# Attention and expert products on one core: another place and bank for the third chunk's second group, and other ranks for the weight conversions

## The chip, the cores and the metric

The kernel runs on one core of a Trainium2 chip. Its engines are TensorE (PE in the profile), VectorE (DVE), ScalarE (ACT), GpSimd (POOL) and SyncE (SP), which here issues the transfers. Each runs its instructions in the order in which they were issued, and semaphores order the engines among each other. The metric is the device time of one execution in microseconds, less being better; times are medians of several runs, and the profile is of one execution.

## The reference

Four sequences of 768 positions, eight heads of 64. Each query sees the keys nearer than 16 positions and, besides, 24 block summaries: a block of 32 keys is represented by its maximum, a block of values by its mean, and log 32 is added to such a score. The result, 3072 rows of 512, goes through two products with 1536 columns, which are multiplied elementwise, and one product back to 512.

```python
k_sum = k.reshape(B, H, nb, block, D).max(axis=3)
v_sum = v.reshape(B, H, nb, block, D).mean(axis=3)
scores_l = scale * np.matmul(q, k.transpose(0, 1, 3, 2))
mask_l = np.abs(pos[:, None] - pos[None, :]) < window
scores_s = scale * np.einsum('bhsd,bhnd->bhsn', q, k_sum) + np.log(block)
a = softmax(concatenate([where(mask_l, scores_l, -1e9), scores_s]))
x = matmul(a, concatenate([v, v_sum]))
...
a = x @ w_a
b = x @ w_b
return (a * b @ w_out).astype(np.float32)
```

(The softmax is written in one line here; the rest is the reference's.)

## The kernel before

**Chunks and groups.** The 3072 rows are cut into 12 chunks of 256 rows (`u` = 0 to 11, three for each sequence), and a chunk into two groups of 128 queries (`i` = 0, 1). Chunk `u` of attention leaves its result in one of two input buffers, `xs[u % 2]`, as a high part and a low part (`x0`, `x1`, halves per group). The expert products of a chunk are 12 items `(u, f)`, one for each 128 hidden columns: 24 matmuls for the two hidden products (L932) and, one item later, 6 for the product back (L968), with two passes of ACT and two of DVE between them (L949 to L957). The items run `(0, f)` and `(1, f)` interleaved, `(0, 11)`, `(1, 10)` and `(1, 11)` last; then `(2, 0)` and on, chunk by chunk. `x0` holds chunk 0's input until `(0, 11)` has read it; then chunk 2's is written there.

**Weights.** The weights arrive as 64-bit numbers, two words each, in 36 parts that are handled in 18 pairs `j`. A conversion of pair `j` (`convert`, L266) takes, for each half, one ACT pass from the raw words into PSUM bank c0 (L289), three DVE steps that go through banks c0 and c1 (L297, L304, L310), an ACT cast (L342) and two POOL passes (L347, L353). All conversions share c0 and c1, so they follow one another. The intermediate numbers lie in scratch spaces: for pairs 0 to 13 in spaces W15 to W17 and S0, for the last four pairs in three slots of two 512-column places each, which are used in rotation, half by half. The raw words of pairs 15, 16 and 17 are loaded into W15, W16 and W17 once these serve no conversion any more; a load further waits for the conversion four pairs earlier.

**Attention.** For chunks 2 and up a group's steps are: queries transposed on DVE (L881), scores on PE into two banks (L583), scaled and masked by DVE into `s` (L608), row maxima (L616), exponentials and sums on ACT (L628), two small DVE steps (L637, L643), scaling on POOL (L658), twelve 32x256 transposes on DVE from `s` into `pt` (L698), products with the values on PE (L712), and the split of the result into a high part by ACT (L720) and a low part by DVE (L723). The place `pt` (`pbuf`) is one for both groups; four of its sixteen blocks stay zero in every group. Chunk 2 (`FILL`) is worked while weights are still being converted: `next(third)` emits its load of queries behind conversion 7, its first group's scores and transposes behind conversion 9, its second group's scores behind conversion 17, and the rest behind item `(0, 11)`. There both groups' products go to bank c0, the second's scores to c0 and c1.

**The next sequence.** Chunk 3 begins a new sequence. Its keys (`prep_keys`, DVE passes L470 to L491) overwrite `kT` after the last scores of chunk 2. Its value means (`prep_values`) are made by POOL (L513) from loads into S1.0 and S1.1, added up in S0.3 and brought into order in S0.2; from there two transfers carry them into `vw`. A space `S0` or `S1` has four places of 512 columns, S0.0 to S0.3.

**The order.** No order is written by hand. Every step is entered in a list (`Work.add`) with its engine, a rank, an estimated duration and the keys that it reads and writes; a step depends on the earlier steps in the list with which its keys collide. `emit` then plays the engines through with the estimates and issues, engine by engine, the step of the lowest rank among those that are ready within 0.15 us; equal ranks are settled by the time at which they became ready. Ranks are 0 for the passes of the expert products, 2 + `j`/4 for conversion `j` (its ACT cast 0.5 less), 2.3 for chunk 1, 5 for chunk 2 (`SOON`), 5.5 for the next keys (`PREP`) and 6 for later chunks and their value means (`LATER`). PE's scores and products of attention have rank -1.

Of the kernel before, what the change touches and what calls it, by code (L numbers as in the profile page):

```python
# [84 lines left out]
def attention_moe(  # L85
# [10 lines left out]
    nc = tc.nc  # L96
    B, H, S, D = q.shape
    P = 128
# [11 lines left out]
    G = CH // P  # L110
    CV = 512
    NW = 3 * NF // 2
    AHEAD = (7, 9, 17)
    FILL = 2

    const = ctx.enter_context(tc.tile_pool(name="const", bufs=1))
# [60 lines left out]
    pbuf = sb([P, 2, NP, P], "pt")  # L177
    vbuf = [sb([P, H, D], f"vw{e}") for e in range(2)]
# [15 lines left out]
    spaces = {n: sb([P, 2048], n) for n in ("S0", "S1")}  # L194
    for j in (*range(8, 13), *range(NW - 3, NW)):
        spaces[f"W{j}"] = wp.tile([P, 2048], F32, tag=f"W{j}", name=f"space{j}")

    kins = [kin, spaces["S1"][:, 2 * CV : 2 * CV + S + 32]]

    def slot(space, i):  # L200
# [18 lines left out]
    def pool(rank, takes, reads, writes, fn):  # L219
        work.add("POOL", rank, takes, 0.1, reads, writes, fn)  # L220
# [8 lines left out]
    CHAIN, FIRST, CONVERT, NEXT, SOON, PREP, LATER = 0, 1, 2, 2.3, 5, 5.5, 6  # L229
# [31 lines left out]
            "SP", rank, 0.45, 524.0, [f"done{j - 4}"] if j > 3 else [], writes, fn, rate=340  # L261
        )

    slots = [("S0", 0), ("S0", 2), ("S1", 2)]

    def convert(j):  # L266
        rank = CONVERT + j / 4
        rk = [f"raw{2 * j}", f"raw{2 * j + 1}"]

        if j < NW - 4:  # L270
            space = {12: "W16", 13: "W17"}.get(j, ("W17", "W16", "W15", "S0")[j % 4])
            places = [(space, 0, 2), (space, 1, 3)]
            single = j < 2
        else:
            places = [slots[(2 * (j - NW + 4) + h) % 3] for h in range(2)]
            places = [(n, x, x + 1) for n, x in places]
            single = True
        cols = [[slice(x * CV, (x + 1) * CV) for x in xs] for _, *xs in places]
        fx, px = [[spaces[places[h][0]][:, cols[h][x]] for h in range(2)] for x in range(2)]
        fk, pk = [[f"{places[h][0]}.{places[h][1 + x]}" for h in range(2)] for x in range(2)]  # L280
        spans = [(h,) for h in range(2)] if single else [(0, 1)]

        def scale(h):
            high = raws[j][:, 2 * h * CV : 2 * (h + 1) * CV].rearrange("p (n t) -> p n t", t=2)
            nc.scalar.activation(  # L289
                bank["c0"], high[:, :, 1].bitcast(F32), AF.Prelu, scale=2.0**-112, alpha=-(2.0**32)  # L290
            )


        def step(n, h):
            f, p, e, s = fx[h], px[h], bank["c0"], bank["c1"]
            if n == 0:
                nc.vector.tensor_scalar(  # L297
                    out=f.bitcast(I32), in0=e.bitcast(I32), scalar1=3, scalar2=None,
                    op0=ALU.logical_shift_left,
                )  # L300
            elif n == 1:


                nc.vector.tensor_scalar(  # L304
                    out=s.bitcast(I32), in0=f.bitcast(I32), scalar1=-(1 << 23), scalar2=None,
                    op0=ALU.bitwise_and,
                )
            else:
                low = raws[j].rearrange("p (n t) -> p n t", t=2)[:, h * CV : (h + 1) * CV, 0]
                nc.vector.scalar_tensor_tensor(  # L310
                    out=p, in0=low.bitcast(U32), scalar=2.0**-52, in1=s, op0=ALU.mult, op1=ALU.mult
                )

        for n, h in [(n, h) for h in range(2) for n in range(3)]:
            f, p, e, s, r = [fk[h]], [pk[h]], ["c0"], ["c1"], [rk[h]]
            if n == 0:
                act(CHAIN, 0.52, r, e, lambda h=h: scale(h))
            reads, writes = ((e, f), (f, s), (r + s, p + [f"done{j}"] + r))[n]
            dve(rank, 0.6, reads, writes, lambda n=n, h=h: step(n, h))

        def parted(part):
            if j not in homes:
                homes[j] = wp.tile([P, 8, 2, P], F32R, tag=f"W{j}", name=f"w{j}")
            return homes[j][:, :, part, :]

        for hs in spans:
            ms = slice(4 * hs[0], 4 * (hs[-1] + 1))
            f, p, hi, lo = (
                [x[h] for h in hs] for x in (
                    fk, pk, [f"hi{2 * j}", f"hi{2 * j + 1}"], [f"lo{2 * j}", f"lo{2 * j + 1}"]  # L330
                )
            )
            x0 = spaces[places[hs[0]][0]]
            f8, p8 = (
                x0[:, cols[hs[0]][x].start : cols[hs[-1]][x].stop].rearrange(
                    "p (m n) -> p m n", n=P
                )
                for x in range(2)
            )
            act(  # L340
                rank - 0.5, 0.25 + 0.37 * len(hs), f + rk, hi,
                lambda ms=ms, f8=f8: nc.scalar.copy(out=parted(0)[:, ms], in_=f8),  # L342
            )
            takes = 0.2 + 1.1 * len(hs)
            pool(
                rank + 0.1 * hs[0], takes, hi, f,
                lambda ms=ms, f8=f8: nc.gpsimd.tensor_tensor(  # L347
                    out=f8, in0=f8, in1=parted(0)[:, ms].bitcast(F32), op=ALU.subtract
                ),
            )  # L350
            pool(
                rank + 0.1 * hs[0], takes, f + p, lo,
                lambda ms=ms, f8=f8, p8=p8: nc.gpsimd.tensor_tensor(  # L353
                    out=parted(1)[:, ms], in0=f8, in1=p8, op=ALU.add
                ),
            )
# [307 lines left out]
    def transposes(u, t, s, sk, banks, diag=None):  # L664
        rank = rank_of(u)
        if u < FILL:
            d, dk = diag

            def turned(h):
                for c in range(NP):  # L670
                    nc.tensor.matmul(
                        bank[banks[h]][:, c * P : (c + 1) * P], s[h][:, c, :], d[:, h, c, :],
                        start=True, stop=True,
                    )

            for h in range(2):
                pe(
                    -1, 0.85, [f"{sk[h]}{c}" for c in range(NP)] + dk[h], [banks[h]],
                    lambda h=h: turned(h),
                )  # L680
                act(
                    rank, 0.6, [banks[h]], dk[h],
                    lambda h=h: nc.scalar.copy(
                        out=d[:, h], in_=bank[banks[h]].rearrange("p (c x) -> p c x", x=P)
                    ),
                )
            return
        sv = sbuf.rearrange("p h c x -> p (h c) x")
        pv = pbuf.rearrange("p h c x -> p (h c) x")


        for i, kb in enumerate(((0, 1, 3), (1, 2, 3), (0, 1, 2), (1, 2, 3))):
            qs = slice(32 * i, 32 * (i + 1))
            for j in kb:
                js = slice(32 * j, 32 * (j + 1))
                dve(
                    rank, 0.45, sk, [f"pt{i}{j}"],
                    lambda js=js, qs=qs: nc.vector.transpose(out=pv[js, :, qs], in_=sv[qs, :, js]),  # L698
                )

# [34 lines left out]
    VK = [f"v{i}" for i in range(5)]  # L735
    s0 = [sbuf[:, h] for h in range(2)]
    SK = ["s0", "s1"]
    PT = [f"pt{i}{j}" for i in range(4) for j in range(4)]

    PD = (pbuf, [[x for x in PT if (x[2] in "01") == (h == 0)] for h in range(2)])  # L740

    def first_attention():
# [113 lines left out]
    def attention(u):  # L856

        b, r = u // NR, u % NR
        rank = rank_of(u)

        banks, vbank = [["c0", "c1"]] * 2, ["c0"] * 2
        if u > FILL:
            banks, vbank = [["c0", "c1"], ["o2", "o3"]], ["c0", "o2"]
        if r == 0:
# [2 lines left out]
        t0 = G * r  # L867
# [10 lines left out]
        def begin(i):  # L878
            dve(
                rank, 0.62, qk, ["qT"],  # L880
                lambda: nc.vector.transpose(out=qTs, in_=qin[:, :, i * P : (i + 1) * P]),  # L881
            )
            scores(
                u, t0 + i, qTs, "qT", s0, SK, banks[i], lead=lead.pop() if lead else None
            )

        def turned(i):
            transposes(u, t0 + i, s0, SK, banks[i])

        def end(i):  # L890
            return u, t0 + i, vbuf, VK, vbank[i]

        if u == FILL:

            yield
            bring(0)
            begin(0)
            turned(0)
            yield
            begin(1)  # L900
            yield
            values(*end(0))
            bring(1)
            turned(1)
            values(*end(1))
        elif u == FILL + 1:
            for i in range(G):
                bring(i)
                begin(i)
                turned(i)  # L910
                values(*end(i))
        else:

            for i in range(G):
                begin(i)
                bring(i)
                turned(i)
                lead.append(products(*end(i)))
# [128 lines left out]
```

## Time and profile before

| | us |
|---|---|
| median of 3 runs | 704.68 (703.55 to 706.06) |
| the profiled execution | 704.12, of which the span is 702.4 |
| PE busy | 682.8 (97%) |
| DVE busy | 436.4 (62%) |
| ACT busy | 252.4 (36%) |
| POOL busy | 181.3 (26%) |
| first hidden product of chunk 2 | starts at 159.17, goes on at 160.90 |
| first hidden product of chunk 3 | 215.29 |

A row of the timeline has the start in us, the duration, the engine, line and operation, what is written from what, shapes and count, and in brackets the idle time of the engine just ahead of it with what ended it. A row of a group has the count, then the busy time, the mean duration in ns, and the idle time ahead of the group. A row of the waits names the waiting line and its releaser, the total in us, how often, and the longest. A row of the stretches has the stretch, its length, then for PE, PE's weight loads, DVE, ACT and POOL the busy time with the number of instructions, then the granted clock (1.00 is full), the share and the GB/s of DMA. The granted clock of the whole execution is 0.998.

### The profile page before, as it was taken

Reading aid. Unit: us, or ns where it says so; the run is one execution under the profiler, and the core shown is the slowest. Engines: PE = TensorE matmul, PEld = TensorE weight load, DVE = VectorE, ACT = ScalarE, POOL = GpSimd, SP = SyncE. Lnnn points to the kernel's source line nnn. Section 1 sums busy time; section 2 is a strip of 40 time slices with the busy share of each in tenths; the row PEclk is TensorE's granted clock in tenths of the full one; section 3 lists DMA queues with packets and bytes.
Section 4 is the critical chain, followed back from the end, with each engine's and each line's share of the span. In section 5 each row is a group of like instructions: output and inputs, shape, how many; then the busy total and the mean of one; then the engine's idle time right before and its main releaser. Section 6 shows DMA issues by size and latency. Waiting matters only on the chain.

```text
span 702.4 us, 15093 instructions
## 1 busy us (share of the span) xinstructions
PE 682.8 (97%) x6000; PEld 626.4 (89%) x6000; DVE 436.4 (62%) x988; ACT 252.4 (36%) x795; POOL 181.3 (26%) x219
## 2 busy tenths in 40 slices
PE   6888999999999999999999999999999999999997
PEld 3778999988999999999999999999999999999996
DVE  2898999797767777666763776762762662311221
ACT  2976574533333314332332323332331431211211
POOL 4378976852433521130110101110110110000000
PEclk9999999999999999999999999999999999999999
DMA  9979773076233335220300330310310100000000
GB/s 229 265 173 309 267 168 126 6 152 145 64 89 96 83 79 107 50 56 19 82 8 17 69 68 2 87 25 1 83 24 1 54 21 1 31 1 1 31 1 31
DMA packets 154943, 54.84 MB, mean 78 GB/s; under 512 B 132456, under 2 KB 147816, under 8 KB 154872
## 3 DMA queue, kind: packets, MB, share of 16 engines
q1 hardware_dynamic: 154872, 53.88, 31.5%
q8 instruction: 47, 0.77, 0.5%
q14 instruction: 24, 0.20, 0.1%
HBM read 47.12 MB, written 6.29 MB: 76 GB/s over the span
## 4 chain that ended last, share of the span: by engine, by line
PE 79%; DVE 7%; POOL 7%; issue 3%; ACT 2%; DMA 2%; SPq 0%; POOLq 0%; ACTq 0%; DVEq 0%
PE h L932 48%; PE o L968 24%; POOL w L353 3%; POOL S L347 2%; DVE c L304 2%; PE o L712 1%; PE c L712 1%; PE o L583 1%; PE c L583 1%; DVE space L297 1%; POOL space L347 1%; DVE space L310 1%; DMA raw<-in_moe_w_b_dram 1%; ACT s L628 1%; DVE ksum L443 1%
## 5 line engine op out<-in xcount | busy, mean ns | idle before, releaser
L932 PEld LDWEIGHTS h<-x,w 128*128 128x128 f32 x3456 | 416.0, 189 | 14.0 <-DVE x L723 2.2
L932 PE MATMUL h<-x,w 128*128 128x256 f32 x3456 | 419.4, 278 | 1.9 <-DVE x L723 1.7
L952 DVE TENSOR_TENSOR h<-h,g 128x256 f32<-128x256 f32 x144 | 62.2, 432 | 164.9 <-ACT g L949 163.2
L968 PE MATMUL o<-w,gh 128*128 128x512 f32 x576 | 157.8, 396 | 1.3 <-ACT gh L954 1.2
L949 ACT COPY g<-h 128x256 f32<-128x256 f32 x144 | 53.8, 374 | 280.8 <-PE h L932 279.9
L968 PEld LDWEIGHTS o<-w,gh 128*128 128x128 f32 x576 | 98.8, 188 | 18.6 <-ACT gh L954 2.3
L698 DVE STREAM_TRANSPOSE pt<-s 32x256 f32<-32x256 f32 x240 | 104.6, 436 | 8.7 <-POOL s L658 4.5
L658 POOL TENSOR_TENSOR s<-s,nml 128x512 f32<-128x512 f32 x40 | 41.6, 1042 | 257.0 <-DVE nml L643 255.5
L968 PE MATMUL o<-w,gl 128*128 128x512 f32 x288 | 90.1, 394 | 0.0
L957 DVE TENSOR_TENSOR gl<-h,gh 128x256 fp32r<-128x256 f32 x144 | 60.7, 422 | 31.6 <-ACT gh L954 30.2
L628 ACT ACTIVATE s<-s,nml 128x128 f32<-128x128 f32 x160 | 62.7, 398 | 43.3 <-DVE nml L616 43.3
L954 ACT CAST gh<-h 128x256 fp32r<-128x256 f32 x144 | 53.6, 372 | 67.6 <-DVE h L952 67.3
L968 PEld LDWEIGHTS o<-w,gl 128*128 128x128 f32 x288 | 53.8, 188 | 11.9 <-issue 0.3
L513 POOL TENSOR_TENSOR S<-S 96x512 f32<-96x512 f32 (+3 forms) x48 | 33.6, 699 | 39.1 <-DMA S<-in_v_dram 30.7
L347 POOL TENSOR_TENSOR space<-space,w 128x1024 f32<-128x1024 f32 (+1 forms) x13 | 26.7, 2056 | 18.8 <-ACT w L342 13.9
L628 ACT ACTIVATION_READ_ACCUMULATOR s<-s,nml 128x1 f32 x160 | 31.1, 194 | 0.0
L289 ACT ACTIVATE c<-raw 128x512 f32<-128x512 f32 x36 | 23.2, 644 | 13.2 <-DVE S L297 5.1
L353 POOL TENSOR_TENSOR w<-space 128x1024 fp32r<-128x1024 f32 (+1 forms) x13 | 26.8, 2059 | 0.9
L637 DVE TENSOR_SCALAR nml<-nml 128x4 f32<-128x4 f32 x40 | 9.8, 244 | 26.9 <-ACT s L628 26.9
L616 DVE TENSOR_REDUCE nml<-s 128x4 f32<-128x512 f32 x40 | 25.4, 669 | 0.0
L409 POOL COPY kT<-ksum 128x144 f32<-128x144 f32 x16 | 4.7, 308 | 61.5 <-DVE ksum L491 54.7
L347 POOL TENSOR_TENSOR S<-S,w 128x512 f32<-128x512 f32 (+1 forms) x11 | 17.6, 1598 | 9.7 <-ACT w L342 9.6
(100 smaller groups left out, 454.2 us busy)
## 6 DMA issues: line engine op xcount, KB each, us to landing
raw<-in_moe_w_a_dram SPq DMA_DIRECT2D x12, 512.0 KB
raw<-in_moe_w_b_dram SPq DMA_DIRECT2D x12, 512.0 KB
raw<-in_moe_w_out_dram SPq DMA_DIRECT2D x12, 512.0 KB
out_dram<-S SPq DMA_DIRECT2D x24, 256.0 KB
qin<-in_q_dram SPq DMA_DIRECT2D x160, 32.0 KB
S<-in_v_dram SPq DMA_DIRECT2D x24, 192.0 KB
vw<-in_v_dram SPq DMA_DIRECT2D x18, 192.0 KB
kin<-in_k_dram SPq DMA_DIRECT2D x24, 100.0 KB
```

The lines of the kernel that those rows point to most:

```text
L347: lambda ms=ms, f8=f8: nc.gpsimd.tensor_tensor(out=f8, in0=f8, in1=parted(0)[:, ms].bitcast(F32), op=ALU.subtract),
L353: lambda ms=ms, f8=f8, p8=p8: nc.gpsimd.tensor_tensor(out=parted(1)[:, ms], in0=f8, in1=p8, op=ALU.add),
L513: lambda: nc.gpsimd.tensor_tensor(out=out, in0=i0, in1=i1, op=ALU.add),
L628: lambda h=h, c=c, sums=sums: nc.scalar.activation(s[h][:, c, :], x[h][:, c, :], AF.Exp, bias=m[:, 0, h, c : c + 1], scale=1.0, accum_out= ...
L658: lambda h=h, r=r: nc.gpsimd.tensor_tensor(out=s[h], in0=s[h], in1=r[:, :, None].broadcast_to([P, NP, P]), op=ALU.mult,),
L698: lambda js=js, qs=qs: nc.vector.transpose(out=pv[js, :, qs], in_=sv[qs, :, js]),
L932: nc.tensor.matmul(ps, w[:, c, part, :], x[xpart][:, c, :], start=(i == 0), stop=(i == n - 1))
L949: act(CHAIN, 0.38, [hk], [gk], lambda: nc.scalar.copy(out=g, in_=pa))
L952: lambda: nc.vector.tensor_tensor(out=pa, in0=pb, in1=g, op=ALU.mult),
L954: act(CHAIN, 0.41, [hk], [ghk], lambda: nc.scalar.copy(out=gh, in_=pa))
L957: lambda: nc.vector.tensor_tensor(out=gl, in0=pa, in1=gh.bitcast(F32), op=ALU.subtract),
L968: nc.tensor.matmul(bank[ok[j]], (gh if first else gl)[:, js], w[:, :, part, :], start=(f == 0 and first and part == 0), stop=(f == NF - 1 ...
```

## The change

- `slots`, the places of the last four conversions, are (S1.0, S0.0, S1.2) instead of (S0.0, S0.2, S1.2). S0.2 and S0.3 serve no conversion after the eleventh; S1.0 and S1.1 do up to the last pair.
- The rank of a conversion is 2 + `j`/6 instead of 2 + `j`/4: 4.0 to 4.83 for pairs 12 to 17 instead of 5.0 to 6.25.
- The second group of chunk 2 turns `s` into a place of its own, `pown` (S0.2 and S0.3, 1024 columns), which POOL sets to zero first. Its transposes have the rank `TURNS` = 5. They are entered in the list ahead of the first group's products instead of behind them.
- That group's products go to bank c1 instead of c0 and read `pown`.

```diff
+    TURNS = 5
...
+    pown = spaces["S0"][:, 2 * CV :].rearrange("p (h c x) -> p h c x", h=2, x=P)
...
-    slots = [("S0", 0), ("S0", 2), ("S1", 2)]
+    slots = [("S1", 0), ("S0", 0), ("S1", 2)]
...
-        rank = CONVERT + j / 4
+        rank = CONVERT + j / 6
...
-        pv = pbuf.rearrange("p h c x -> p (h c) x")
+
+        own = u == FILL and t % G == 1
+        dst, key = (pown, "pu") if own else (pbuf, "pt")
+        pv = dst.rearrange("p h c x -> p (h c) x")
+        rank = TURNS if own else rank
...
-                    rank, 0.45, sk, [f"pt{i}{j}"],
+                    rank, 0.45, sk + ["S0.2"] * own, [f"{key}{i}{j}"],
...
+    PU = [f"pu{i}{j}" for i in range(4) for j in range(4)]
...
-        banks, vbank = [["c0", "c1"]] * 2, ["c0"] * 2
+        banks, vbank = [["c0", "c1"]] * 2, ["c0", "c1"] if u == FILL else ["c0"] * 2
...
-            return u, t0 + i, vbuf, VK, vbank[i]
+            pt = (pown, [PU, ["S0.2", "S0.3"]]) if u == FILL and i else None
+            return u, t0 + i, vbuf, VK, vbank[i], pt
...
             begin(1)
+            pool(rank, 0.9, (), ["S0.2", "S0.3"], lambda: nc.gpsimd.memset(pown, 0.0))
+            turned(1)
             yield
             values(*end(0))
             bring(1)
-            turned(1)
             values(*end(1))
```

## The prediction

> **What bounds the kernel now.** First the page: busy time by engine, and PE in 40 slices of 17.6 us; then PE's own waits from 100 to 215 us, the two longest.
>
> ```profile
> PE 682.8 (97%) x6000; PEld 626.4 (89%) x6000; DVE 436.4 (62%) x988; ACT 252.4 (36%) x795; POOL 181.3 (26%) x219
> ...
> PE   6888999999999999999999999999999999999997
> ...
> PE h L932 <- DVE x L723: 1.3, 1, 1.3
> PE o L968 <- ACT gh L954: 0.6, 1, 0.6
> ```
>
> PE is the bound: 97%, and nine tenths or more in every slice from the fifth (70 us) to the last but one. Every matmul of before is still there after, so a gain can come only out of PE's lost time. The two waits make 1.9 us, but groups that drag don't appear as waits. So I count the work against the clock. The timeline gives the price of a hidden product (24 matmuls), an output product (6) and a group of attention matmuls (32); the stretches view counts matmuls on either side of 138.72 us, where the third chunk's second group puts its scores on PE.
>
> ```profile
> 93.82 2.91 PE L932 MATMUL h<-x,w 128*128 128x256 f32 x24
> 96.56 1.08 PE L968 MATMUL o<-w,gh 128*128 128x512 f32 x4
> ...
> 97.94 0.76 PE L932 MATMUL h<-x,w 128*128 128x256 f32 x5
> ...
> 138.72 1.23 PE L583 MATMUL c<-kT,qT 64*64 64x128 f32 x32
> ...
> 187.00 2.91 PE L932 MATMUL h<-x,w 128*128 128x256 f32 x24
> 189.83 1.15 PE L712 MATMUL c<-pt,vw 128*64 128x64 f32 x32
> 190.92 0.97 PE L968 MATMUL o<-w,gh 128*128 128x512 f32 x3
> ...
> 118.54:138.72 20.18, 19.96 (x145) 18.47 (x144) 17.51 (x32) 10.27 (x22) 15.31 (x12) 1.00 0.09 35
> 138.72:160.90 22.18, 19.86 (x200) 16.73 (x199) 19.71 (x50) 9.29 (x30) 11.43 (x15) 1.00 0.68 142
> ```
>
> Starts give 96.56 - 93.82 = 2.74 us for a hidden product, 97.94 - 96.56 = 1.38 for an output product, and 190.92 - 187.00 - 2.74 = 1.18 for a group with its switches. The first stretch holds 144 matmuls of its own: five hidden and four output products, 5 x 2.74 + 4 x 1.38 = 19.2 us of 20.18, so 1.0 lost. The second holds, of its 200, 72 in three hidden products and one more (0.1 us), 30 in five output products and 96 in three groups: 8.2 + 0.1 + 6.9 + 3.5 = 18.7 of 22.18, so 3.4 lost. **4.4 us** in all is what better order can give here. Both losses have one origin, seen on POOL and DVE:
>
> ```profile
> 103.72 1.04 POOL L658 TENSOR_TENSOR s<-s,nml 128x512 f32<-128x512 f32 x1 [1.18 <-DVE nml L643]
> 104.72 2.41 POOL L347 TENSOR_TENSOR space<-space,w 128x1024 f32<-128x1024 f32 x1
> 107.50 1.04 POOL L658 TENSOR_TENSOR s<-s,nml 128x512 f32<-128x512 f32 x1 [0.38 <-DVE nml L643]
> ...
> 122.06 1.30 POOL L347 TENSOR_TENSOR S<-S,w 128x512 f32<-128x512 f32 x1 [6.04 <-ACT w L342]
> 127.90 1.30 POOL L347 TENSOR_TENSOR S<-S,w 128x512 f32<-128x512 f32 x1 [0.54 <-ACT w L342]
> 144.96 0.32 POOL L513 TENSOR_TENSOR S<-S 96x64 f32<-96x64 f32 x1
> ...
> 96.30 1.27 DVE L616 TENSOR_REDUCE nml<-s 128x4 f32<-128x512 f32 x2
> ...
> 109.84 1.77 DVE L698 STREAM_TRANSPOSE pt<-s 32x256 f32<-32x256 f32 x4
> 116.67 0.69 DVE L297 TENSOR_SCALAR S<-c 128x512 int32<-128x512 int32 x1
> 138.13 0.68 DVE L310 SCALAR_TENSOR_TENSOR S<-raw,c 128x512 f32<-128x512 uint32 x1
> 148.20 0.87 DVE L698 STREAM_TRANSPOSE pt<-s 32x256 f32<-32x256 f32 x2
> 155.77 0.44 DVE L698 STREAM_TRANSPOSE pt<-s 32x256 f32<-32x256 f32 x1
> 160.17 0.68 DVE L723 TENSOR_TENSOR x<-c,x 128x512 fp32r<-128x512 f32 x1
> ```
>
> The reader sees DVE spend 109.84 to 116.67 on the first group's twelve transposes before conversion 14 begins; POOL, done with conversion 13 at 122.06 - 6.04 = 116.02, stands still for 6.04 us. The last conversions drag to about 144.9 (the add L513, which waits for their space, starts at 144.96), and the second group's scores, which need bank c1 from the last conversion (L310 ends at 138.81), come at 138.72. Its transposes run from 148.20 to 156.21 and its split ends at 160.85 (L723): there PE waits, to 160.90, with one matmul of chunk three's first hidden product done.
>
> **The change part by part.** *Ranks* (2 + j/4 becomes 2 + j/6). Conversions 12 to 17 go from 5.0..6.25 to 4.0..4.83, ahead of the third chunk (5) and the next keys (5.5). POOL's 6.04 us gap closes, and its two 1.04 us scalings with their waits of 1.18 and 0.38 no longer stand between conversions 11 and 13: 6.0 + 3.6 = 9.6 us at most. They, and the memset, come back in the short gaps (0.54) that the rotation of three slots leaves, at about 0.5 each, 1.5 together. Conversions then end near 144.9 - 9.6 + 1.5 = 137, bounds 135 and 139 (139 if only the 6.04 goes). The last L310 precedes that end by 6.1 us, so c1 is free near 131 and the scores run on PE at about 132 instead of 138.72.
>
> *What is pushed back.* The first group's softmax and transposes fall behind 36 conversion steps on DVE. The sum on DVE from 96.3 us, where the first group's L616 stood, to the last split, beside the rows of above:
>
> ```profile
> L304 DVE TENSOR_SCALAR c<-S 128x512 int32<-128x512 int32 x14 | 9.7, 690 | 0.2
> L952 DVE TENSOR_TENSOR h<-h,g 128x256 f32<-128x256 f32 x144 | 62.2, 432 | 164.9 <-ACT g L949 163.2
> L637 DVE TENSOR_SCALAR nml<-nml x6: 149/226/1648, 101.7 to 175.4; 128x4 f32<-128x4 f32 x6
> L153 POOL MEMSET mask<- 128x384 f32 x1 | 0.4, 418 | 0.0
> ```
>
> 36 x 0.69 = 24.8; 24 transposes at 1.77 / 4 = 0.44, 10.6; six large passes (four L616, two L608) at 1.27 / 2 = 0.64, 3.8; eight small steps 1.4; two splits and an output copy at 0.68, 2.0: 42.6 us. The expert products take two passes of 0.43 from every 2.74 + 1.38 = 4.12 us, so the floor is 42.6 / 0.79 = 53.9, ending at 150.2. By the chain instead: first group's transposes finish near 138, the second's reductions near 140, and from the end of the scores to the first transpose stood 148.20 - 139.95 = 8.3 us before; I take first transpose near 145, last near 152 (8.0 us of before less the output copy), products on PE at the next boundary, about 153, and split ended three later, near 156. PE without its 4.4 us loss would be at the corresponding matmul at 160.90 - 4.4 = 156.5. So they meet; x has 0.5 us in hand, but the products can enter PE only between two groups, half a hidden product (1.4) later on average, so I leave PE 0.9 of its loss. **Gain 3.5**, bounds 1 (x ready at 159 and the same 0.9) and 4.4.
>
> *Own place and bank.* The transposes write S0.2/S0.3, the products c1, so neither waits for the first group's products. That costs one memset of 1024 columns: 418 ns for 384 makes about 1.0 us on POOL, hidden in a gap, 1.0 on the conversions if it isn't. TURNS is 5, the rank these transposes already had: nothing. The 12 transposes, 32 matmuls and the three loads of values keep their count and their queue; the loads still wait for the first group's products.
>
> *Slots.* S1.0/S1.1 now serve conversions, so two loads of values for the next sequence leave the early DMA queue:
>
> ```profile
> 43.28 0.91 SPq L225 DMA_DIRECT2D S<-in_v_dram x2
> ...
> 54.23 1.04 PE L712 MATMUL o<-pt,vw 128*64 128x64 f32 x28 [0.66 <-DMA vw<-in_v_dram]
> 59.09 1.05 ACT L342 CAST w<-space 128x1024 fp32r<-128x1024 f32 x1
> 60.12 5.62 PE L932 MATMUL h<-x,w 128*128 128x256 f32 x47 [0.31 <-DVE x L723]
> ```
>
> PE waits 0.66 and 0.31 behind later loads: up to 1.0 gained if they come forward. Against it, the new ranks put cast L342 of conversion 4 (2.5 to 2.17) ahead of the second chunk's split (2.3), 1.05 us on the same chain. I take 0, bounds -1.0 and +1.0. The moved loads wait for conversion 17's first half (near 134), and the last add of their pair, 144.96 before, waits for the second group's products, near 154: 9 us later. What it delays is off PE's path as long as this slack lasts:
>
> ```profile
> 185.18 1.83 SPq L225 DMA_DIRECT2D vw<-S x2
> 201.28 0.69 DVE L723 TENSOR_TENSOR x<-o,x 128x512 fp32r<-128x512 f32 x1
> 215.29 2.91 PE L932 MATMUL h<-x,w 128*128 128x256 f32 x24
> ```
>
> The fourth chunk's input is ready at 201.97 and used at 215.29, 211.8 after a gain of 3.5: 9.8 us of slack, of which 9 at most are used.
>
> Sum: 704.12 - 3.5 = 700.6 for the profiled execution; that lies 0.56 under the median 704.68, so 701.2 for a median.
>
> [...] L637's row: 149 ns at least, 1648 at most. The two long ones:
>
> ```profile
> 101.69 0.88 DVE L637 TENSOR_SCALAR nml<-nml 128x4 f32<-128x4 f32 x1
> 105.50 1.65 DVE L637 TENSOR_SCALAR nml<-nml 128x4 f32<-128x4 f32 x1
> ```
>
> The second ends at 107.15, and POOL's pass beside it (L347 from 104.72) at 107.13: DVE stood until POOL finished. [...]
>
> **Rivals.**
> (1) *DVE holds x back.* The first group's two L637 meet a full POOL: 2 x 2.41 less the 2.2 already paid is 2.6 us more on DVE; x at 156 + 2.6 = 158.6, 2.1 after PE. With the 0.9 left as before, the gain is 4.4 - 3.0 = 1.4: 703.3. For it: DVE is busy for 17.51 of the 20.18 us before 138.72 already. [...]
> (2) *Nothing gained.* The last conversions wait for their raw weights instead, as their spaces come free only with POOL's passes 12 and 13, or the early cast takes back 1.05 and DVE the rest: 704.7. Against: conversions 12 and 13 end earlier too.
> (3) *Slower.* The sums of the next sequence. Their add waits for the second group's products (+9), and their loads may then queue on SP behind sixteen query loads:
>
> ```profile
> 170.64 8.86 SPq L225 DMA_DIRECT2D qin<-in_q_dram x16
> ```
>
> That makes 9 + 8.9 = 18; the slack decides from 9.8, so PE stands 8.1 us before chunk four and the kernel is 8.1 - 3.5 = 4.6 slower: 709.3. Against: the 9 alone don't use up the slack, and the sixteen loads need to fall on the chain again.
>
> **How the numbers follow.** A measurement of this kernel can tell about 0.3% (2.1 us) from no change: faster is under 702.6, slower over 706.8. Forecast 0.58 (699.4 to 702.5), rival 1 0.22 (mostly 702.6 to 704), rival 2 0.08, rival 3 or another late input 0.12. With 0.03 of rival 1 counted as faster: 0.61, 0.27, 0.12. The range takes gain 4.4 + 1.0 at one end, 699.3, and rivals 1 and 2 at the other, 705.0; it leaves out 0.12 above and a little below.
>
> **What would show it.** Right: POOL's 6.04 us gap gone, last conversion done near 137, second group's scores near 132, its products near 153, no wait on L723 over 0.5 us, the start of the chunk-four products near 212. Wrong: L637 steps over 1 us inside the last conversions and L723 again releasing PE (rival 1); ACT waiting for raw weights (2); PE waiting for vw, or for chunk four's split (3); new idle time on PE before 60 us.

## The result and the profile after

| | median us | runs | ratio to the kernel before |
|---|---|---|---|
| before | 704.67 (703.02 to 706.91) | 15 | |
| after | 699.54 (698.61 to 703.56) | 15 | 0.9934 [0.9921, 0.9947] |

The medians lie 5.1 us apart, 0.66% by the ratio. The profiled execution of after took 699.38 us (span 697.7), 4.74 us less than that of before. In after the lines have moved on: L225 to L658 by two, L698 to L723 by six, L932 to L983 by nine.

The page of after, busy time by engine and PE in 40 slices; then PE's own waits from 62 us to the end, all of them:

```profile
PE 680.6 (98%) x6000; PEld 625.5 (90%) x6000; DVE 434.9 (62%) x988; ACT 252.7 (36%) x795; POOL 181.8 (26%) x220
...
PE   5889999999999999999999999999999999999997
```

```profile
PE o L977 <- ACT gh L963: 0.7, 1, 0.7
```

PE does the same 6000 matmuls, and its wait on the split of chunk 2 (1.3 us before) is gone. The timeline of POOL:

```profile
110.61 1.32 POOL L349 TENSOR_TENSOR S<-S,w 128x512 f32<-128x512 f32 x1
...
115.88 0.96 POOL L909 MEMSET S<- 128x1024 f32 x1
117.33 1.31 POOL L349 TENSOR_TENSOR S<-S,w 128x512 f32<-128x512 f32 x1 [0.49 <-DMA qin<-in_q_dram]
...
122.61 1.05 POOL L660 TENSOR_TENSOR s<-s,nml 128x512 f32<-128x512 f32 x1
...
133.86 1.29 POOL L355 TENSOR_TENSOR w<-S 128x512 fp32r<-128x512 f32 x1
...
153.00 0.32 POOL L515 TENSOR_TENSOR S<-S 96x64 f32<-96x64 f32 x1 [8.53 <-DVE S L704]
```

The stop of 6.04 us at 116 is gone. The memset lies among the conversions, the last of which ends at 135.15 instead of about 144.9. PE and DVE in the same execution:

```profile
129.42 1.10 PE L585 MATMUL c<-kT,qT 64*64 64x128 f32 x32
...
138.87 1.15 PE L718 MATMUL c<-pt,vw 128*64 128x64 f32 x32
...
152.51 1.47 PE L718 MATMUL c<-S,vw 128*64 128x64 f32 x32
...
156.79 5.63 PE L941 MATMUL h<-x,w 128*128 128x256 f32 x48
...
208.13 5.63 PE L941 MATMUL h<-x,w 128*128 128x256 f32 x48
```

```profile
144.50 1.33 DVE L704 STREAM_TRANSPOSE S<-s 32x256 f32<-32x256 f32 x3 [0.25 <-POOL s L660]
...
151.55 1.35 DVE L704 STREAM_TRANSPOSE S<-s 32x256 f32<-32x256 f32 x3
152.93 0.69 DVE L729 TENSOR_TENSOR x<-c,x 128x512 fp32r<-128x512 f32 x1
...
155.02 0.68 DVE L729 TENSOR_TENSOR x<-c,x 128x512 fp32r<-128x512 f32 x1
```

The second group's scores come at 129.42 (138.72 before) and its products at 152.51. The split ends at 155.70, 1.1 us ahead of the hidden product that needs it (156.79). Chunk 3's first hidden product is the second half of the group at 208.13, so about 210.87.

**Where the time went.** Cut the execution at two places with the same work between them in every kernel of this study but one (e12, see there): the start of item (1, 4)'s hidden product (93.82 in before, 93.62 after) and the start of chunk 2's first one (160.90 with one matmul done, so 160.78, before; 156.79 after). Between them lie 14 hidden products, 15 output products and three groups of attention: 14 x 2.745 + 15 x 1.375 + 3 x 1.18 = 62.6 us of work. What is above 62.6 is PE's loss.

| | until (1, 4) | stretch | lost in it | from there to the end |
|---|---|---|---|---|
| before | 93.82 | 66.96 | 4.4 | 541.6 |
| after | 93.62 | 63.17 | 0.6 | 540.9 |

3.8 of the 4.7 us come from this stretch, 0.2 from ahead of it, 0.7 from behind it.

### The profile page after: what moved, and what is told of

It reads as the page before. It is cut to its first block, busy times and chain, and to the rows that moved or that the text cites. A ratio compares the mean times of both kernels' runs of the same rounds, so it can differ in the third digit from the quotient of the medians.

```text
span 697.7 us, 15101 instructions
## 1 busy us (share of the span) xinstructions
PE 680.6 (98%) x6000; PEld 625.5 (90%) x6000; DVE 434.9 (62%) x988; ACT 252.7 (36%) x795; POOL 181.8 (26%) x220
## 4 chain that ended last, share of the span: by engine, by line
PE 91%; DVE 4%; ACT 2%; DMA 1%; issue 1%; POOL 0%; SPq 0%; POOLq 0%; ACTq 0%
PE h L941 55%; PE o L977 29%; PE c L718 2%; PE c L585 2%; PE o L718 2%; PE o L585 1%; DMA raw<-in_moe_w_b_dram 1%; PE o L673 1%; ACT s L630 1%; DVE ksum L445 1%; DVE S L704 1%; DVE space L299 1%; PE o L573 1%; DVE c L306 1%; DVE space L312 0%
## 5 line engine op out<-in xcount | busy, mean ns | idle before, releaser
L704 DVE STREAM_TRANSPOSE pt<-s 32x256 f32<-32x256 f32 x228 | 99.4, 436 | 7.6 <-POOL s L660 3.4
L639 DVE TENSOR_SCALAR nml<-nml 128x4 f32<-128x4 f32 x40 | 8.0, 201 | 30.3 <-ACT s L630 30.3
```

## The experiments

The theory behind the prediction: DVE's early transposes of the first group stop POOL and so the last conversions, and the ranks cure that; place and bank are worth little by themselves. The rival: place and bank carry the gain. Every kernel was timed against the kernel before on the same chip. The last column is the loss in the stretch defined above, in the one profiled execution; the ratios' intervals are some 1 us to either side; the loss resolves more finely, but is of a single execution.

| kernel | ranks | own place | bank c1 | median us | ratio | lost us |
|---|---|---|---|---|---|---|
| before (first chip) | | | | 704.39 | | 4.4 |
| ranks alone (e1) | yes | | | 699.89 | 0.9929 [0.9915, 0.9944] | 1.3 |
| place and bank (e2) | | yes | yes | 700.42 | 0.9948 [0.9930, 0.9966] | 2.1 |
| ranks and place (e3) | yes | yes | | 699.34 | 0.9924 [0.9910, 0.9939] | 0.5 |
| late ranks only, all else (e4) | from pair 12 | yes | yes | 701.23 | 0.9946 [0.9931, 0.9961] | 1.0 |
| before (second chip) | | | | 703.84 | | |
| place alone (e7) | | yes | | 704.36 | 0.9995 [0.9977, 1.0013] | 3.2 |
| bank alone (e8) | | | yes | 701.51 | 0.9966 [0.9949, 0.9984] | 2.4 |
| transposes later (e9) | | | | 700.84 | 0.9945 [0.9927, 0.9963] | 2.2 |
| the change, other casts (e10) | yes | yes | yes | 701.73 | 0.9958 [0.9939, 0.9976] | 0.6 |
| before (third chip) | | | | 704.77 | | |
| ranks and bank (e11) | yes | | yes | 699.03 | 0.9929 [0.9909, 0.9949] | 0.4 |
| transposes later and bank (e12) | | | yes | 701.29 | 0.9953 [0.9938, 0.9968] | 2.1 |

### The ranks alone

```diff
-        rank = CONVERT + j / 4
+        rank = CONVERT + j / 6
```

> Only the ranks of the conversions change (2 + j/6); slots, place and bank are those of before. Theory A (the ranks bring the gain, because POOL's 6 us stop goes and the second group's scores come some 8 us earlier): 3 us or more faster than before, near 701, scores of the second group at 129 to 133 us. Theory B (the place and the bank bring it, the ranks alone only move work): under 1.5 us faster, 703 to 705.

699.89 us: one expression does the whole gain that can be measured. POOL's stop is down to 0.66 us and the second group's scores are at 129.39. In the stretch PE keeps one wait; its timeline and DVE's:

```profile
153.96 1.15 PE L712 MATMUL c<-pt,vw 128*64 128x64 f32 x32 [0.93 <-DVE x L723]
```

```profile
153.21 0.69 DVE L723 TENSOR_TENSOR x<-c,x 128x512 fp32r<-128x512 f32 x1
```

The products of the second group wait until DVE has read the first group's out of bank c0 (153.90).

### Place and bank without the ranks

The change, with this line as it was:

```diff
-        rank = CONVERT + j / 6
+        rank = CONVERT + j / 4
```

> Slots, own place and bank c1 as in the changed kernel, the ranks of before (2 + j/4). Theory A: under 1.5 us faster than before, 703 to 705, POOL's 6 us stop still there. Theory B: 3 us or more faster, near 701.

700.42 us, against the theory behind the prediction: POOL stands still as before, and yet more than half of the gain is there.

```profile
119.14 1.30 POOL L349 TENSOR_TENSOR S<-S,w 128x512 f32<-128x512 f32 x1 [5.92 <-ACT w L344]
```

```profile
136.35 1.10 PE L585 MATMUL c<-kT,qT 64*64 64x128 f32 x32
...
153.74 1.03 PE L718 MATMUL c<-S,vw 128*64 128x64 f32 x28 [0.42 <-DVE S L704]
...
156.88 5.61 PE L941 MATMUL h<-x,w 128*128 128x256 f32 x47 [0.41 <-DVE x L729]
```

So a slow POOL alone doesn't make the loss. Look at what the products waited for in the kernel before, on DVE and on PE:

```profile
155.77 0.44 DVE L698 STREAM_TRANSPOSE pt<-s 32x256 f32<-32x256 f32 x1
156.22 0.69 DVE L723 TENSOR_TENSOR x<-c,x 128x512 fp32r<-128x512 f32 x1
```

```profile
156.20 1.21 PE L968 MATMUL o<-w,gh 128*128 128x512 f32 x4 [0.61 <-ACT gh L954]
157.33 1.15 PE L712 MATMUL c<-pt,vw 128*64 128x64 f32 x32
```

The last transpose ends at 156.21, but c0 is free only at 156.91, after the first group's split. In PE's order an output product, itself 0.61 us late, stands ahead of them here, and the products run at 157.33. Which part of e2 cured this, its place or its bank, is what e7 and e8 ask.

### The change with bank c0

```diff
-        banks, vbank = [["c0", "c1"]] * 2, ["c0", "c1"] if u == FILL else ["c0"] * 2
+        banks, vbank = [["c0", "c1"]] * 2, ["c0"] * 2
```

> The changed kernel, but the second group's products go to bank c0 as before. In the changed kernel the first group's result leaves c0 only with the DVE split at 152.93 to 153.6 us, and the second group's products start at 152.51. If the bank counts, the products wait for that split and x comes 1 to 2 us later: 700.5 to 701.5, PE waiting for DVE's split at chunk two's first hidden product. If it doesn't: 699.5, like the changed kernel.

No cost: 699.34 us. PE and DVE show why:

```profile
153.25 1.15 PE L718 MATMUL c<-S,vw 128*64 128x64 f32 x32
```

```profile
152.50 0.69 DVE L729 TENSOR_TENSOR x<-c,x 128x512 fp32r<-128x512 f32 x1
```

The bank is free at 153.19, and PE, whose row of an output product ends at 153.11, takes the products at 153.25: here the bank is hardly waited for. In e1, with bank c0 too but without the place, it was, for 0.93 us.

### The new rank from pair 12 on only

```diff
-        rank = CONVERT + j / 6
+        rank = CONVERT + (j / 4 if j < 12 else j / 6)
```

> The changed kernel with 2 + j/4 for conversions 0 to 11 and 2 + j/6 from 12 on. Theory A: only the last six conversions count, 699 to 700.2. Theory C (the early ranks gave the part of the gain that the forecast did not have, by another order before 65 us): 700.5 to 701.5.

701.23 us lies where theory C had put it, but the ratio, 0.9946 against 0.9934 of the whole change, doesn't settle it: the intervals overlap. The scores come at 129.81 and 1.0 us is lost in the stretch instead of 0.6, so the ranks of pairs 12 to 17 do most of the work there; whether the earlier ones add something isn't settled.

### The place alone

e2 with the line of e3.

> The change without the new rank of the last conversions (old rank everywhere) and with the second group's products in bank c0: only the place of their transposes is new. If the bank is what helped the run with the places alone, the products of the second group wait for VectorE's split of the first group again (about 0.5 to 1 us at 153 to 157), and the gain over the kernel before falls to 1 to 3 us: 702 to 703. If the place is what helps, it is like the run with both places: about 700.4. The stop of POOL of some 6 us at 116 to 123 stays in both.

704.36 us, a ratio of 0.9995: nothing, where either case of the expectation had a gain of at least 1 us. (The one profiled execution lost 1.2 us less in the stretch than that of before, but at 702.53 us it is among the fastest of its kernel; the medians show none of it.) The rows suggest why: nobody waits for the place. In before the first group's products, at 141.44 on PE, have read `pt` by 142.59, 5.6 us ahead of the second group's first transpose (148.20), and in after they do so by 140.02, ahead of 144.50.

### The bank alone

The kernel before, with

```diff
-        banks, vbank = [["c0", "c1"]] * 2, ["c0"] * 2
+        banks, vbank = [["c0", "c1"]] * 2, ["c0", "c1"] if u == FILL else ["c0"] * 2
```

> The kernel before with only the second group's products of the third chunk in bank c1: no new place, no new rank. If the bank frees these products from VectorE's split of the first group, they come right after the transposes, about 1.5 to 2.3 us earlier: 702.1 to 702.9. If it is the place, nothing changes: 704 to 705.

701.51 us, 2.4 us by the ratio, a little more than was expected if the bank counts. POOL's stop is untouched, the products come with the transposes, beside the split of the first group instead of behind it, and of the wait for x little is left. POOL, DVE and PE:

```profile
120.64 1.30 POOL L347 TENSOR_TENSOR S<-S,w 128x512 f32<-128x512 f32 x1 [6.04 <-ACT w L342]
```

```profile
154.89 0.69 DVE L723 TENSOR_TENSOR x<-c,x 128x512 fp32r<-128x512 f32 x1
...
156.95 0.65 DVE L723 TENSOR_TENSOR x<-c,x 128x512 fp32r<-128x512 f32 x1
```

```profile
154.92 1.03 PE L712 MATMUL c<-pt,vw 128*64 128x64 f32 x28 [0.20 <-DVE pt L698]
...
157.38 5.89 PE L932 MATMUL h<-x,w 128*128 128x256 f32 x48
```

The second split follows the products' end (155.95) by 1.0 us; in before it followed (158.48, then 160.17) by 1.7. PE shows no wait for x, but the split ends at 157.60, and inside PE's last row here a weight load waits 0.31 us for it: the row takes 5.89 us instead of 5.62.

### Only the first group's transposes later

The kernel before, with one line ahead of the transposes, so that they fall behind conversion 14:

```diff
+        rank = 6.3 if u == FILL and t % G == 0 else rank
```

> The kernel before, with only the twelve transposes of the first group ranked later, behind conversion 14's part of VectorE: the conversions, their places and banks are untouched. If the stop of POOL at 116 to 122 comes from VectorE doing these transposes first, the stop goes, the second group's scores come about 5 us earlier (133 to 134 instead of 138.7) and 2 to 3.5 us are gained: 701.2 to 702.7. If the stop has another cause, or the query loads that stand behind the conversions matter more, it stays within 1 us of the kernel before.

700.84 us: with the conversions' own ranks as they were, the stop shrinks from 6.04 to 0.48 us and the second group's scores begin 6.8 us earlier (1.8 of these lie ahead of the stretch: item (1, 4) starts at 92.04 here), on POOL and PE:

```profile
114.73 1.31 POOL L347 TENSOR_TENSOR S<-S,w 128x512 f32<-128x512 f32 x1 [0.48 <-ACT w L342]
```

```profile
131.96 0.43 PE L583 MATMUL c<-kT,qT 64*64 64x128 f32 x4
133.29 1.09 PE L583 MATMUL c<-kT,qT 64*64 64x128 f32 x28 [0.90 <-DVE S L310]
```

This is the cause named in the prediction, isolated: twelve transposes on DVE stop POOL. It takes away half of the loss (4.4 to 2.2); the scores now wait 0.90 us for the last conversion, and the first group's products 0.50 behind them.

### Later transposes and the bank together

> The kernel before with the first group's transposes ranked behind conversion 14's part of VectorE, and bank c1 for the second group's products. The two did 3.9 and 2.4 us by themselves. If they take the same loss away, they don't add: 700 to 701, as with the transposes alone. If they take different parts of the 4.4 us of PE's loss, the loss is nearly gone: 698.5 to 699.5, as with the change or better.

e9's line and e8's together: 701.29 us, and 2.1 us lost, as with the transposes alone (one output product lies behind the stretch here, 1.4 us, and is counted in). The two gains don't add: 3.9 and 2.4 us alone, 3.3 together, worked out from the ratios, whose intervals overlap. They are two ways to be in time for the same event: in e9 the first group's split has freed c0 at 150.78, ahead of the second group's products at 152.84, so another bank has nothing left to cure, and both kernels show the waits of 0.90 and 0.5 us around the scores.

### Ranks and bank, without the place

> The kernel before with the new ranks and with bank c1 for the second group's products, without the place of their own (and so with the old slots). If the place adds nothing beside the ranks, it is like the change, 699 to 700, and the wait of 0.9 us on the split of chunk 2 that the ranks alone had at 153 is gone. If the place matters there, the second group's transposes wait for the first group's products: 1 to 2 us slower than the change, 700.5 to 701.5.

The kernel before with the lines of e1 and e8: 699.03 us, 0.9929, like the change, with the old slots, without the place and its memset. The list of PE's waits is empty from 62 us on. It is the smallest edit that leaves no loss to speak of (0.4 us); that it is faster than the change isn't shown.

### A try at something better

The change, with the lead of 0.5 in rank that a conversion's ACT cast has left to the first two conversions alone, so that chunk 1's exponentials, for which PE waits 2.02 us at 44, come ahead of the third's cast:

```diff
-                rank - 0.5, 0.25 + 0.37 * len(hs), f + rk, hi,
+                rank - (0.5 if j < 2 else 0), 0.25 + 0.37 * len(hs), f + rk, hi,
```

> The change, with ACT's cast of the first two conversions ranked half a place earlier against the exponentials, so that chunk 1's exponentials come ahead of the third conversion's cast. If the wait of PE of 2.0 us at 44 to 46, and the low granted clock in the 3 us behind it, are paid for in the sum, the time falls by 1 to 2 us: 697.5 to 698.5. If PE is merely held somewhere else in the start (each conversion must be there before the products that use it), it stays at 699.5, and the wait only moves.

701.73 us, not faster than the change. The wait at 44 us is 0.83 instead of 2.02, and others take its place:

```profile
49.23 1.44 PE L941 MATMUL h<-x,w 128*128 128x256 f32 x10 [1.67 <-POOL w L355]
...
56.97 1.72 PE L977 MATMUL o<-w,gh 128*128 128x512 f32 x4 [2.72 <-DVE x L729]
```

Item (1, 4) starts at 95.39 instead of 93.62. Ahead of 60 us PE is held by the conversions and by chunk 1's input, and a step put forward delays another.

## Why the prediction was right, and where it was off

It said 701.2 us (699.3 to 705.0) and faster; 699.54 was measured, just inside the lower end. The profiled execution gained 4.74 us where the sum had 3.5; of the 1.2 us between, 0.3 came from the stretch that the sum is about, and 0.9 from ahead of it and behind it, which no term of the sum explains.

- *PE's lost time is the ceiling, 4.4 us.* Right as the size of the stretch's loss, of which 3.8 came back; the whole gain is above it by what came from outside the stretch.
- *Ranks.* Right. The stop closes, the last conversion ends at 135.15 (137 forecast, bounds 135 and 139), the scores are at 129.42 (132). e1 shows that the ranks are enough, e9 that the transposes on DVE were what stopped POOL.
- *Pushed back.* Right to within 1 us: second group's transposes from 144.50 to 152.90 (145, 152; the output copy that was to drop out stayed among them, at 150.39), products at 152.51 (153), x at 155.70 (156), with 1.1 us in hand instead of 0.5. I left PE 0.9 us of its loss, and 0.6 was left: a gain of 3.8 here instead of 3.5.
- *One origin for both losses.* This step was incomplete. The stop of POOL makes the scores late, but nearly half of the loss came from the bank: with c0 the products had to wait behind DVE's split of the first group, as e8 shows, where the stop stays and 2.0 of 4.4 us come back in the profiled execution. I had read the rows of the last transpose (155.77) and of the last split (160.17), and not the first group's split between them (156.22).
- *Own place and bank at nothing.* Right for the change as it is (e3 and e11 against after: no difference), though not because such edits are free of effect: the bank alone is worth 2.4 us, which the ranks have already taken. With the ranks alone PE still waits 0.93 us for bank c0 (e1, 1.3 us lost against 0.4 in e11); the ratios, 0.9929 for both, don't show it. The memset ran between conversions; the place alone gave nothing in the medians.
- *Slots at nothing, bounds of 1.0.* Item (1, 4) starts 0.2 us earlier. This start lies anywhere from 91.44 to 95.39 in the twelve profiled executions, and 1.9 us apart for two kernels in which ACT and POOL have the same order up to there (e2 92.11, e4 94.01), so it says nothing about the slots. The place alone, which brings the new slots with it, gave no difference.
- *Not in the sum:* the 0.7 us behind chunk 2's first hidden product. 0.26 of it lies in the group of 47 matmuls at 160.90 in before, which takes 5.64 us to the next start, where 47 of 48 of two hidden products (5.49) make 5.38; why isn't shown (in e7 the same 47, behind a wait of 0.98 us, take 5.45). The remaining 0.4 isn't settled either: this part takes 540.9 to 542.2 us in the executions of this study (e12 without its output product), with no order in it that follows the edits.
- *Rival 1, DVE held by POOL at L637.* It fell: L639 took 0.16 and 0.24 us among the last conversions. That such a step is held for a whole pass of POOL, 2.41 us, as this rival's sum takes it, is shown by no run; the two longest shown took 1.65 us in before and 1.66 in e9. DVE was held all the same in e2, where two steps took 1.24 and 1.34 us; DVE and POOL there:

```profile
98.21 1.24 DVE L639 TENSOR_SCALAR nml<-nml 128x4 f32<-128x4 f32 x1
103.26 1.34 DVE L639 TENSOR_SCALAR nml<-nml 128x4 f32<-128x4 f32 x1
```

```profile
97.02 2.41 POOL L355 TENSOR_TENSOR w<-S 128x1024 fp32r<-128x1024 f32 x1
102.16 2.42 POOL L349 TENSOR_TENSOR space<-space,w 128x1024 f32<-128x1024 f32 x1
```

Both DVE steps end 0.02 us behind the POOL pass beside them (99.45 and 99.43, 104.60 and 104.58). In after the passes are halves of 1.3 us and the steps met their last 0.1 to 0.2. That was luck in part: with halves too, one step took 0.98 us in e1, and two took 1.25 and 1.16 in e4, about as much as in before, each ending 0.02 to 0.03 behind work of POOL.
- *Rival 2, waits for raw weights.* It didn't come: the waits of ACT between 94 and 140 us in after name PE and DVE, and no transfer.
- *Rival 3, the sums of the next sequence.* Its first half came: the add is at 153.00 instead of 144.96 (8.0 us later, 9 forecast), the transfer of the sums into `vw` starts at 190.38 instead of 185.18, and chunk 3's input is ready at 205.77 instead of 201.97. Its price did not: chunk 3's (the prediction's fourth chunk's) first hidden product is at 210.87 (about 212 forecast), so 5.1 us of slack remain.

## What to carry to other kernels

When a stop and a loss stand near each other, look for a second condition on the same path before calling the one the origin: here the late scores and the shared bank were both needed for the full loss, and curing either got a good part of it back (3.1 of 4.4 us by the ranks, 2.0 by the bank), so the gains didn't add. Price an edit together with what the others leave of the loss: a free edit beside a good one may be a gain by itself, and the other way round. And ask of each new buffer who had waited for the old one; here the rows showed nobody, and the medians no gain.

## What was not expected of the hardware

PE's granted clock fell behind a wait of 2.02 us, which before and after have alike, to 46 us. The stretches by single microseconds, of before and then of after:

```profile
46.00:47.00 1.00, 0.97 (x9) 1.00 (x10) 1.00 (x3) 0.94 (x6) 1.00 (x1) 1.00 0.46 98
47.00:48.00 1.00, 1.00 (x8) 1.00 (x7) 0.93 (x4) 1.00 (x5) 0.94 (x1) 0.62 0.91 291
48.00:49.00 1.00, 1.00 (x7) 1.00 (x6) 0.96 (x3) 0.94 (x6) 0.60 (x1) 0.50 0.99 373
...
50.00:51.00 1.00, 1.00 (x7) 1.00 (x7) 1.00 (x3) 0.38 (x1) 0.92 (x2) 0.68 1.33 252
```

```profile
46.00:47.00 1.00, 0.99 (x6) 1.00 (x7) 1.00 (x3) 0.93 (x6) 1.00 (x1) 0.74 1.01 380
...
49.00:50.00 1.00, 1.00 (x7) 1.00 (x7) 0.88 (x4) 0.97 (x5) 0.00 (x0) 0.55 1.37 217
50.00:51.00 1.00, 1.00 (x10) 1.00 (x10) 0.97 (x3) 0.71 (x1) 0.21 (x1) 1.00 1.32 207
```

The clock column (the first behind the five engines) goes down to 0.50, half speed, and reads as a stretch of 3.4 us in both: 47.24 to 50.64 in before (0.76 of the microsecond at 47, 0.64 of that at 50, two whole ones), 46.48 to 49.90 in after. It begins 0.8 us earlier in after, although the wait ends at the same time. e10 fits a link to the wait: behind its waits of 0.83 and 1.67 us there the clock stayed at 1.00, and behind its wait of 2.72 us, to 56.97, it was 0.72, 0.50, 0.50 and 0.58 in the microseconds from 57 on, 3.4 us of half speed again (a mean of 0.86 from 50 to 62). What sets the length and the start of such a stretch isn't shown. Half speed for 3.4 us cost about 1.7 us of matmul time, by an estimate from these rows (half of 3.4, PE being busy): in before the hidden product from 46.91 on, in which the whole stretch lies, takes 4.45 us to the next start, 1.7 more than the 2.745 of others. The stretch stands at this place in both kernels, so it isn't part of the difference.
